# Sixteen groups of zero products put into a fixed order of steps, three taken out

## The chip, the cores and the metric

The kernel runs on one core of a Trainium2 chip. The core has a matrix engine (TensorE, PE in the profile, with its weight loads as PEld), a vector engine (VectorE, DVE), a scalar engine (ScalarE, ACT), a general engine (GpSimd, POOL) and a queue that issues transfers (SyncE, SP). Each works off its own instructions in order and waits on semaphores for the others. The metric is the device time of one execution in microseconds; lower is better, and of several runs the median counts.

## The reference

Two blocks stand behind each other, in float32. The first is a delta rule over 768 steps in time for 4 batches of 8 heads of 48 features; the second mixes over the sequence and then over the channels.

```python
k_n = k / (np.linalg.norm(k, axis=-1, keepdims=True) + 1e-06)
for t in range(S):
    y[:, :, t] = einsum('bhd,bhde->bhe', q[:, :, t], state)
    v_old = einsum('bhde,bhd->bhe', state, k_n[:, :, t])
    state += beta[:, :, t] * outer(k_n[:, :, t], v[:, :, t] - v_old)
x = y.transpose(0, 2, 1, 3).reshape(4, 768, 384)
u = x + (relu(x.transpose(0, 2, 1) @ w_tok1) @ w_tok2).transpose(0, 2, 1)
out = u + relu(u @ w_ch1) @ w_ch2
```

Here w_tok1 is 768x256, w_tok2 256x768, w_ch1 384x1536 and w_ch2 1536x384. They come as 64-bit numbers and are rounded on the core.

## The kernel before

**Tiling.** The recurrence is cut into units of 128 positions of one batch (24 units u), each of two chunks of 64. For each unit the kernel loads keys and queries (job k, `load_kq`), normalises and transposes them (p, `prep`: the transposes are L562 and L582, ScalarE copies them out of PSUM in L566 and L587), forms the products of keys with keys and queries (c and d, `grams`, L511, and their masking on VectorE, L517), inverts a unit triangular matrix of each chunk (t, i, f, h, j: to parts, the elimination on VectorE in L755 and L760, back, and the joining of parts by small products, L790, L803, L864, L905), loads the values (v), and runs the recurrence over the chunks (r, `recur`: L933, L940, L957, L963, L971 and L972, L980, L985). Units 0 to 5 pass the inversion in SBUF; later ones go through DRAM on the way in and out (n_dram and w_dram). Four units share one inversion.

**The second block** is job m for batches 0 and 1 (`mixer`: L1606, L1621, L1681, L1702) and T, A, F, B for batches 2 and 3, which run at the end. The weights are rounded piece by piece (w0 to w33, `round_weights`: a load in L280, ScalarE in L286 and L287, VectorE in L289, GpSimd in L293). Job b loads beta (L252), turns it on TensorE into p_b (L257) and copies it to beta_st on ScalarE (L261).

**The order.** Each job is a Python generator; `next` issues its instructions up to the next yield. What comes when is written out by hand: the string `order` (L1788) is a list of steps, `k0*6` being six steps of job k0, and the loop at L1861 issues them one by one. The tile framework is told to keep this order, so on each engine the instructions stand in the order of the string. A step that waits holds up all that is behind it on its engine.

**Zero products.** Three jobs multiply zeros by zeros into a PSUM tile of their own, p_warm, that nobody reads: x and z take one product of 128x128 by 128 or by 512 columns, Y (and y, the same generator) takes four of 64x64 by 128 columns that lie in the four quarters of the array. In float32 each product is two matmul instructions in the trace, so an x or a z is two and a Y eight.

```python
def keep_warm(m):
    zero = warm[:, 0:128]
    while True:
        nc.tensor.matmul(p_warm[:, 0:m], zero, zero[:, None, :].to_broadcast([128, m, 128]))
        yield
def warm_tiles():
    while True:
        for j in range(2):
            for r in PAR:
                nc.tensor.matmul(p_warm[r, j], warm[r, 0:C], warm[r, 0:128])
        yield
```

Of the kernel before, what the change touches and what calls it, by code (L numbers as in the profile page):

```python
# [23 lines left out]
def kernel(  # L24
# [41 lines left out]
    B, H, S, D = q.shape  # L66
# [117 lines left out]
    t11 = const.tile([128, NB, HB], FP32, name="t11")  # L184
# [17 lines left out]
    w1 = const.tile([128, NCH, DTOK], FP32, name="w1")  # L202
    w2 = const.tile([128, NDH, S], FP32, name="w2")
# [407 lines left out]
    t16 = spare[:, cuts[1] : cuts[2]].rearrange("s (q t b) -> s q t b", q=2, t=QB)  # L611
# [1182 lines left out]
    w13*2 w6*2 k5*2 v0 k6 k5*2 i0*2 d4*2 k5 x z d4*3 c4 z*2 p5*2 k5 t4 p5 h0 h1  # L1794
    h0 w8*2 h1 Y i0 f0 Y p4 f1 h2*2 p5*3 f0*2 w6 h0*5 k6*5 p6 z f2*2 k8*3 p5 w6
    p5 p3 p5 j0*3 f1*2 h1*5 j0*2 w8*2 w17 f2 h2*3 v0 w17 r0*5 p6 h2*2 c5*2 v1
    w11*2 j1 p5 k7*2 c5 k7 c5 r0 c5 r0*2 w14*2 v1 w11*2 k7*2 p7 d5*5 r1*5 w14*2
    p6*2 t5 j1 r1*2 j1 j2 p7 h3*2 r1*3 p6*3 i1*2 r2*5 k8*2 f3*2 w9 k9*3 j1*2 v2*2
    i1*3 j2*2 r2*2 f3 i1*2 p6*3 w16 v2 w16*3 r2*2 h3 r2 i1 d6 r3*5 i1*2 w9*3 v2
    d6 h3 v2 w0 h3*2 r3 h3 d6*2 w0 d6 j3 c6*5 r3*4 w0 j2 w0 p8*2 j2 r4 p8 r4*4  # L1800
    k9*3 j3*2 r4*2 i1*2 w24 i1*2 p7*7 r4 c7 r4 r5*5 k10 p9 k10 p9 c7 r4 c7*3 i1
    w5*2 p7 r5*2 w24*3 r5*3 j3*2 i1 r6*4 w26 v3*5 p9 k11 r6 d7*5 w26*3 p8*3 t6*2
    r6*2 w5*2 p8*4 v4*2 t6 i1 r6*3 h5*2 h4*2 k10*2 f4*3 c8*2 k10 p10 w28*2 c8*2
    r7 c8 r7*3 d8*4 p9 d8 w28 h4*5 p9 t6 r7*2 j4 w28 p9*3 r7*2 p9 w7 d9 w7 v4*2
    f5*2 w27*2 w7*2 d9*4 c9*2 f5 c9*3 t7*2 t8 r7*2 t7*2 j4*2 v4 p10*2 h5 r8*3 w29
    t8*3 w29 w27*2 r8*2 w29*2 q3 w29 j4*2 r8 w22*4 t9*3 r8*3 p9 r9 p10 r9*3 t9 v5
# [36 lines left out]
    m1*2 p23*3 m1*3 p23*5 v18 r29 p22 f18 m1*3 c23*3 f20*2 f18 c23 f18*2 c23
    f19*3 v18 r30 t22*4 c23 t23 r30*4 t23*3 f20 m1*3 i6 j18*3 f19 m1*2 S m1 j19*2
    j20 j19 f21 r29*2 f21 i6*4 m1*3 i6*6 j20*2 m1 r30*3 m1*2 r30*2 i6 f21 m1*2
    r30 r31*4 r28 r30*2 i6 j21 f20 j21*2 i6*2 r31*3 v20 i6 v20*2 i6 m1*2 i6*3
    r31*4 f21 j21 i6*2 v22*3 v20*2 r32*5 r31 r29 r31*2 i6*3 m1*5 j21 m1 r32 v21*2
    r32 i6*7 m1*2 r30 r32*6 v21*2 s v21 s v22 m1*4 v22 s f22 f23 f22*3 r33*5
    f23*2 j22 m1*4 r33*3 v23 j22 r33*2 j22 W j23*2 T2 r33*2 T2 f23 r33 l s l s
    r33 j23 r34*4 j23 r34*2 W*3 v23*4 j23 r34*2 T2 r32 r34*5 r35*8 T2 r35*2 T3 W  # L1850
    r35*2 l*2 T3 s*5 W*2 T2*5 s r34 r35 A0*7 T2*3 A0*11 S*3 A0*6 l s l s A0*18 A1
    A0*4 A1*2 A0*3 S*3 A0*20 A1*2 T3*2 F0*5 T3*10 A1 S T3 A1*3 T3*3 B0 T3*8 B0*3
    T3*4 B0 T3 A1*5 T3*3 A1*2 B0*2 A1*6 W A1*3 F0 A1*6 F0 A1*4 B0 A1*15 A2 F0
    A1*3 A2*2 A1*9 F0*2 A1*14 W*3 A2*3 B0*2 A2*5 B0*3 W*2 F0 B0*3 F1 F0 B0*2 F0*2
    B0 A1 B0*4 F0 F1*2 B0*6 A2*10 B1 F1*2 A2*7 B1 A3*2 A2*3 B0 A2*26 A3 A2*12 F1
    A2*2 F1*4 B1*4 A2*5 A3 F1 F2 A3 B1*4 A3*6 F1*2 B1*7 F1 B1*2 A2 F2*3 F1 B1*6
    B2 A3*10 B1*3 A3*15 B1 A3*26 F2*4 A3*3 F2*3 B1 B2*4 A3*7 B2*5 A3 B2*2 A3*4
    F2*2 F3 B2*7 F3*2 B2*2 F3*2 B2 F3*3 B2*6 F3 F2*2 B3*2 F3 B3*10 F3 B2*2 B3*5
    F3*4 B3*13
    """  # L1860
    for word in order.split():  # L1861
        name, _, n = word.partition("*")
# [34 lines left out]
```

## Time and profile before

| what | value |
|---|---|
| median of three runs | 619.56 us (616.66 to 621.06) |
| the profiled execution | 617.85 us, span 616.1 us |
| mean granted TensorE clock | 0.983 |
| TensorE, VectorE, ScalarE, GpSimd busy | 588.7, 468.3, 253.8, 107.5 us |
| zero products | x36 instructions of x and z (L235), x48 of Y (L245) |
| steps in the order | 2598, of which 8 are x, 10 z, 6 Y |

Three views are used beside the page. A window gives the busy time of every engine in a stretch, the granted clock and the DMA share (the numbers with an x are counts of instructions). The chain of waits goes back from the last instruction to what released it, step by step. The timeline lists instructions in the order of time, with the idle time of the engine ahead of one and what ended it in square brackets: `[1.30 <-PE p_b L257]` is 1.30 us idle, ended by TensorE's p_b. Times in them count from the start of the span. "Cold" is not a word of the profile: the column PEclk has the share of the clock that was granted, and 0.50 is half.

### The profile page before, as it was taken

Reading aid. Unit: us, or ns where it says so; the run is one execution under the profiler, and the core shown is the slowest. Engines: PE = TensorE matmul, PEld = TensorE weight load, DVE = VectorE, ACT = ScalarE, POOL = GpSimd, SP = SyncE. Lnnn points to the kernel's source line nnn. Section 1 sums busy time; section 2 is a strip of 40 time slices with the busy share of each in tenths; the row PEclk is TensorE's granted clock in tenths of the full one; section 3 lists DMA queues with packets and bytes.
Section 4 is the critical chain, followed back from the end, with each engine's and each line's share of the span. In section 5 each row is a group of like instructions: output and inputs, shape, how many; then the busy total and the mean of one; then the engine's idle time right before and its main releaser. Section 6 shows DMA issues by size and latency. Waiting matters only on the chain.

```text
span 616.1 us, 21239 instructions
## 1 busy us (share of the span) xinstructions
PE 588.7 (96%) x8733; PEld 513.6 (83%) x8733; DVE 468.3 (76%) x1506; ACT 253.8 (41%) x676; POOL 107.5 (17%) x144
## 2 busy tenths in 40 slices
PE   9488988999999999999999999999999999999998
PEld 5467775667898988977889898896699999999997
DVE  4996876986799754797567977967788898775874
ACT  7659885457521344222651305424252332414200
POOL 3147364134411112013020120010000000000000
PEclk9979897999999999999999999998999999999999
DMA  9577657647542344354435343144102012020001
GB/s 220 112 160 166 166 145 199 160 115 183 109 110 65 85 106 82 92 122 103 104 71 136 84 99 63 35 87 117 34 0 40 1 22 56 1 53 13 14 27 51
DMA packets 154608, 55.55 MB, mean 90 GB/s; under 512 B 129648, under 2 KB 148976, under 8 KB 154512
## 3 DMA queue, kind: packets, MB, share of 16 engines
q1 hardware_dynamic: 154512, 54.20, 37.9%
q8 instruction: 68, 1.11, 0.8%
q14 instruction: 28, 0.23, 0.1%
HBM read 41.19 MB, written 11.21 MB: 85 GB/s over the span
## 4 chain that ended last, share of the span: by engine, by line
PE 81%; DVE 10%; ACT 5%; issue 2%; DMA 1%; SPq 0%; ACTq 0%; DVEq 0%
PE p_c L1681 16%; PE p_r L1511 13%; PE p_o L1702 13%; PE p_a L1583 7%; PE p_b L1583 6%; PE p_g L511 3%; PE p_h L1621 3%; PE p L1606 2%; DVE sub L755 2%; DVE x L760 2%; PE p L1236 2%; PE p_y L1047 1%; PE p_warm L235 1%; PE p_h L1251 1%; PE p_k L933 1%
## 5 line engine op out<-in xcount | busy, mean ns | idle before, releaser
L1681 PE MATMUL p_c<-u_t,wc 128*128 128x256 f32 x432 | 101.6, 386 | 0.3 <-issue 0.3
L1681 PEld LDWEIGHTS p_c<-u_t,wc 128*128 128x128 f32 x432 | 79.6, 190 | 11.7 <-issue 0.8
L755 DVE TENSOR_TENSOR sub<-x 128x56 f32<-128x56 f32 (+41 forms) x351 | 71.1, 243 | 4.4 <-DMA x<-n_dram 2.3
L760 DVE TENSOR_TENSOR x<-x,sub 128x56 f32<-128x56 f32 (+41 forms) x351 | 69.0, 237 | 0.2
L1702 PE MATMUL p_o<-wc,r 128*128 128x192 f32 x360 | 64.3, 330 | 0.2 <-DVE xb L1641 0.2
L1702 PEld LDWEIGHTS p_o<-wc,r 128*128 128x128 f32 x360 | 58.4, 190 | 1.5 <-DVE xb L1641 0.5
L1690 ACT ACTIVATE r<-p_c 128x512 f32<-128x512 f32 x36 | 21.5, 596 | 52.2 <-PE p_c L1681 46.4
L511 PE MATMUL p_g<-kq 48*64 48x128 f32 (+1 forms) x704 | 33.5, 280 | 3.3 <-ACT kq L587 3.3
L517 DVE TENSOR_TENSOR gm<-p_g,mb 128x512 f32<-128x512 f32 x44 | 28.9, 684 | 7.5 <-PE p_g L511 7.0
L574 POOL TENSOR_TENSOR mb<-mask_c,cs 128x512 f32<-128x512 f32 x20 | 21.4, 1068 | 71.3 <-DVE cs L552 41.7
L484 POOL TENSOR_TENSOR v_st<-v_st,nrm 128x384 f32<-128x384 f32 x12 | 11.3, 944 | 126.5 <-DMA v_st<-in_v_dram 97.7
L293 POOL TENSOR_TENSOR wc<-w_f,d 128x384 uint32<-128x384 uint32 x24 | 24.7, 1031 | 42.2 <-DVE w_f L289 17.0
L511 PEld LDWEIGHTS p_g<-kq 48*64 48x64 f32 (+1 forms) x704 | 25.7, 136 | 6.1 <-ACT kq L587 4.3
L1511 PE MATMUL p_r<-t_d,wc 128*128 128x192 f32 x160 | 28.8, 326 | 0.0
L1524 DVE TENSOR_TENSOR kq<-kq,p_r 128x384 f32<-128x384 f32 x40 | 21.1, 552 | 10.0 <-PE p_r L1511 8.1
L1524 DVE TENSOR_TENSOR gm<-gm,p_r 128x384 f32<-128x384 f32 x40 | 21.1, 552 | 8.1 <-PE p_r L1511 5.8
L1511 PEld LDWEIGHTS p_r<-t_d,wc 128*128 128x128 f32 x160 | 26.5, 190 | 0.0
L400 DVE STREAM_TRANSPOSE kq<-pads 128x512 f32<-128x512 f32 x24 | 25.4, 1105 | 1.0 <-PE p_y L1047 0.6
L1702 PE MATMUL p_o<-wc,s 128*128 128x192 f32 x144 | 25.7, 330 | 0.0
L1511 PE MATMUL p_r<-pads,wc 128*128 128x192 f32 x128 | 25.4, 326 | 0.0
L1702 PEld LDWEIGHTS p_o<-wc,s 128*128 128x128 f32 x144 | 23.3, 190 | 0.6 <-DVE xb L1641 0.3
L1511 PE MATMUL p_r<-t_d,lent 128*128 128x192 f32 x128 | 23.7, 326 | 0.0
(311 smaller groups left out, 1362.2 us busy)
## 6 DMA issues: line engine op xcount, KB each, us to landing
d<-in_moe_w_ch_dram SPq DMA_DIRECT2D x24, 384.0 KB, 3.8
v_st<-in_v_dram SPq DMA_DIRECT2D x96, 48.0 KB, 2.8
out_dram<-xb SPq DMA_DIRECT2D x23, 192.0 KB, 1.9
kst<-in_k_dram SPq DMA_DIRECT2D x64, 48.0 KB, 2.4
n_dram<-gm SPq DMA_DIRECT2D x72, 32.0 KB, 1.7
pads<-in_k_dram SPq DMA_DIRECT2D x24, 96.0 KB, 2.3
pads<-in_q_dram SPq DMA_DIRECT2D x24, 96.0 KB, 3.4
gm<-w_dram SPq DMA_DIRECT2D x72, 32.0 KB, 2.3
```

Of the source, the lines that this page charges most:

```text
L293: nc.gpsimd.tensor_tensor(out=dst.bitcast(U32), in0=f, in1=lo, op=ALU.add)
L400: nc.vector.transpose(kq_of[p // 2][:, i, :, p % 2].rearrange("f p (s g) -> f p g s", g=G), rows_of[i].rearrange("s p (g d) -> s p g d", g ...
L511: nc.tensor.matmul(p_g[PAR[i ^ cc ^ swap(u)], p], kqt[f, p, cc, 0], kqt[f, p, cc])
L517: nc.vector.tensor_tensor(out=blocks(gm_of(u))[:, :, cc, D:GW].rearrange("s p (two n) -> s p two n", two=2), in0=p_g, in1=made[u][:, :, cc ...
L755: nc.vector.tensor_tensor(out=half, in0=by[0].to_broadcast(list(to.shape)), in1=by[1].to_broadcast(list(to.shape)), op=ALU.mult,)
L760: nc.vector.tensor_tensor(out=to, in0=to, in1=half, op=ALU.add)
L1511: nc.tensor.matmul(p[:, i], pieces[q // width][:, at : at + 128], f[f"u{n}"], start=first and i == 0, stop=True, skip_group_check=True,)
L1524: nc.vector.tensor_tensor(out=o, in0=o, in1=p, op=op_of(sign))
L1583: nc.tensor.matmul(p, a[:, i], w[:, i // 2, i % 2], start=first and i == 0, stop=True, skip_group_check=True,)
L1681: nc.tensor.matmul(p_c[:, k], piece_of(wc1, cb, f * 128)[:, f * 128 : (f + 1) * 128], u_t[:, cb], start=(cb == 0), stop=(cb == NCB - 1),)
L1690: nc.scalar.activation(r2[:, m], p_c, ACTF.Relu)
L1702: nc.tensor.matmul(p, a[:, m], wc2[:, m, j], start=(start and i == 0), stop=(i == NM - 1), skip_group_check=True,)
```

## The change

Only the string `order` differs. Among all its steps but x, z and Y the order is the same. One x and one z go from the start, and one z moves a step ahead (counted as one out and one in). Otherwise come in: nine Y, two x, and four z, three of these behind each other. The new order has 2611 steps.

| at about (us in the trace of before) | before | after |
|---|---|---|
| 2 to 4 | `w10 x*4 z w10*2` | `w10 x*3 w10*2` |
| 12 | `p0*2 z w3` | `p0 z p0 w3` |
| 22 | `p3*7 c3` | `p3*6 Y p3 c3` |
| 25 | `i0*2 w13` | `i0*2 z*3 w13` |
| 43 | `i0 f0 Y p4` | `i0 f0 Y*2 p4` |
| 47 | `j0*3 f1*2` | `j0 Y j0*2 f1*2` |
| 50 | `w8*2 w17` | `w8 Y w8 w17` |
| 58 | `p6*3 i1*2` | `p6 Y p6*2 i1*2` |
| 64 | `r2*2 h3` | `r2 Y r2 h3` |
| 69 | `r3*4 w0` | `r3*2 x r3*2 w0` |
| 79 | `d7*5 w26*3` | `d7*4 z d7 w26*3` |
| 94 | `r8*3 w29` | `r8 Y r8*2 w29` |
| 101 | `h5*3 j5` | `h5 x h5*2 j5` |
| 110 | `j5 i2*3 p10` | `j5 Y i2*3 p10` |
| 138 | `f7 m0 w29` | `f7 Y m0 w29` |

In the source the lines of the string are filled anew, so that many of them shift. Its first lines:

```diff
     order = """
-    w10 x*4 z w10*2 z w1*4 k1*3 z k1*3 z b p1 z p1 k0*6 p0*2 b*2 p1 w2 p0*5 p1*2
-    w10 p0*2 z w3 w2 c0*3 p0 w3*2 d0*2 w3 c0 p1 c0 d0*3 k2*3 v1 p1*2 w18 k2*2
+    w10 x*3 w10*2 z w1*4 k1*3 z k1*3 z b p1 z p1 k0*6 p0*2 b*2 p1 w2 p0*5 p1*2
+    w10 p0 z p0 w3 w2 c0*3 p0 w3*2 d0*2 w3 c0 p1 c0 d0*3 k2*3 v1 p1*2 w18 k2*2
     p1*2 c1*2 d1 k2 p2*2 c1 t0 d1 c1*2 d1*3 p2*8 c2*2 w2 d2 c2*3 Y d2 w2 k3*6 p3
-    d2*2 p3 d2 t1 x p3*7 c3 k4*5 k7 w13 w18*2 d3*2 v1*2 v0*2 c3*3 v0 c3 d3*3 p4*2
-    t2 x t3 p4*2 x i0*2 w13 p4*2 w18 w17*2 i0 k4 i0*9 p4 i0*2 p4*2 c4 k8 c4*3
...
+    d2*2 p3 d2 t1 x p3*6 Y p3 c3 k4*5 k7 w13 w18*2 d3*2 v1*2 v0*2 c3*3 v0 c3 d3*3
+    p4*2 t2 x t3 p4*2 x i0*2 z*3 w13 p4*2 w18 w17*2 i0 k4 i0*9 p4 i0*2 p4*2 c4 k8
...
```

More of the change, by code (lines that the diff above doesn't have):

```diff
@@ L1800 @@
[L1800 to L1806, printed above, removed]
@@ L1856 @@
[L1856 to L1859, printed above, removed]
+    d2*2 p3 d2 t1 x p3*6 Y p3 c3 k4*5 k7 w13 w18*2 d3*2 v1*2 v0*2 c3*3 v0 c3 d3*3
+    p4*2 t2 x t3 p4*2 x i0*2 z*3 w13 p4*2 w18 w17*2 i0 k4 i0*9 p4 i0*2 p4*2 c4 k8
+    c4*3 w13*2 w6*2 k5*2 v0 k6 k5*2 i0*2 d4*2 k5 x z d4*3 c4 z*2 p5*2 k5 t4 p5 h0
@@ new lines @@
+    h1 h0 w8*2 h1 Y i0 f0 Y*2 p4 f1 h2*2 p5*3 f0*2 w6 h0*5 k6*5 p6 z f2*2 k8*3 p5
+    w6 p5 p3 p5 j0 Y j0*2 f1*2 h1*5 j0*2 w8 Y w8 w17 f2 h2*3 v0 w17 r0*5 p6 h2*2
+    c5*2 v1 w11*2 j1 p5 k7*2 c5 k7 c5 r0 c5 r0*2 w14*2 v1 w11*2 k7*2 p7 d5*5 r1*5
+    w14*2 p6*2 t5 j1 r1*2 j1 j2 p7 h3*2 r1*3 p6 Y p6*2 i1*2 r2*5 k8*2 f3*2 w9
+    k9*3 j1*2 v2*2 i1*3 j2*2 r2*2 f3 i1*2 p6*3 w16 v2 w16*3 r2 Y r2 h3 r2 i1 d6
+    r3*5 i1*2 w9*3 v2 d6 h3 v2 w0 h3*2 r3 h3 d6*2 w0 d6 j3 c6*5 r3*2 x r3*2 w0 j2
+    w0 p8*2 j2 r4 p8 r4*4 k9*3 j3*2 r4*2 i1*2 w24 i1*2 p7*7 r4 c7 r4 r5*5 k10 p9
@@ new lines @@
+    w4 i2 j5 Y i2*3 p10 v5 r9*2 d10*3 r10 v7*2 j5 i2*2 r10*4 w12 i2 k12 i2*2 m0
+    w32 k11 k12 w32 r10*2 m0 p11 k12*4 w19 p11 r10 c10 r10 c10 r10 w33 d10*2 q2 Y
+    r11*4 v7 r11*3 w19 c10 q1 w30 c10 r11 k12*2 i2*3 r11 v6*4 i2*5 m0*3 i2*5 q5
+    i2 m0 p11*4 c10 p11 m0 p11*2 m0*2 k12*2 w12 m0*3 v6 f6*3 w12 d11 c11*2 d11*2
+    c11 w33 c11 d11*2 j6 p12 w12 m0 w33 w30*3 p12*2 f7*3 j6*2 m0 c11 j7 f6 f8
+    w27*2 f8 j7 f8 w15 f7 Y m0 w29 w33 w29 j7 r12*4 w31 j8 p11 t10*3 r12 Y r12 f9
+    j8 f9 w21 p12 r12 f8 r13*2 w15*2 r12 w15 r13*3 w31*3 Y r13*2 w33 j8 w21 m0
@@ new lines @@
+    r13 q4 p12*4 r13*2 m0*2 r14 c12 f9 j9 r14*2 w21 t10 w20*2 v7 r14*2 c12*2 w33
+    c12 r14 v8 c12*2 r14*2 w25*2 j9 r14 r15 v8 w21 r14 r15 w25 r15*3 w25 k13*4
+    w20 k13*4 p13 k13*2 w20 v8*3 m0*2 p13 w25 p13 m0 r15 p13 r15 p13 w27 w25
+    k13*2 j9 m0*4 p13 f9 w23 t12*3 p13 t12 w25 r15*3 c13*6 w23 k14*7 r16*5 m0 p13
+    m0*3 w23*4 k14 r16*2 t11 t13*2 j9*2 t11*3 w33 p14 r16*2 p14*2 w31 m0*3 w31 m0
+    w31 m0 w23 r17*2 r16 t13 r17 t13 r17*2 p14*2 m0*2 p14 i3 k14*4 i3*3 k15 v9*2
+    m0*3 v10 i3*5 k15 i3 r17 k15*2 p14 k15*3 m0 v10*2 i3 k15*2 m0*2 k15*2 i3*4
@@ new lines @@
+    r17*4 k15 i3*2 p14 m0*2 i3*6 m0*4 r18 i3 r18*2 v9*3 r18*2 i3*8 m0*10 v10*2 m0
+    r18 c14*4 r18*2 m0*2 f10 c14 f10*2 f12*2 p15*3 m0*4 r18 r19 r18 r19*3 j10 f10
+    j10*2 f12 p15 f11*4 f12 r19 c14 r19 v11 p15*3 k16*7 j11 m0*2 r19*4 j11 j12
+    r20*3 k16*2 r20 m0 r20 k16*3 v11 m0 j11 r20*2 v11*2 p15 c15*2 p10 r20*2 c15
+    r20 c15*3 f13*3 p16 r21*5 m0 r21*2 p16*4 k17*7 p16 j12*2 p16 k17 r21*3 m0*3
+    r22 c16 r22*3 k17*4 v11 r22 c16*4 r22*2 m0 r22 t14 p17 f13 c16 t14 j13*2 t14
+    r22 r23 t15*2 t16 r23*2 r22 r23 m0*3 r23 t15*2 r23 p17*5 t16 p17 j13 t16*2
@@ new lines @@
+    r27*2 p20*2 k20*2 p20 c19*2 r26*2 k20 v16*2 r25 c19 m1*2 f17 r27*4 p20 k20
+    p20 j17*2 m1 r27*5 c20*4 p20 r28*4 c20*2 k21*9 p21*2 k21*2 p21 k21 m1*2 v16
+    r28 t18 v17 p21*5 t19*4 t18*2 j17 t18 j17 m1*2 r28*3 c21*6 m1*3 r28*3 m1*2
+    r28 m1 t20 s t20*3 t21*4 i5 m1*4 i5 v17*2 r26 i5*2 m1*2 r28 k22*3 i5*4 k22*6
+    m1*2 i5*2 m1*3 i5 v17 r29 i5*3 p22*2 i5 r29 v17 r29*3 i5*2 v19 p22*3 k22*3
+    m1*4 r29 v19*2 i5 k23*6 p22 v18 p22 i5*11 k23*4 r29*2 k23 i5 k23 v18*2 i5*2
+    v19 m1*7 v19 m1*5 r29 c22*5 r29 r27 c22 m1*2 p23*3 m1*3 p23*5 v18 r29 p22 f18
@@ new lines @@
+    m1*3 c23*3 f20*2 f18 c23 f18*2 c23 f19*3 v18 r30 t22*4 c23 t23 r30*4 t23*3
+    f20 m1*3 i6 j18*3 f19 m1*2 S m1 j19*2 j20 j19 f21 r29*2 f21 i6*4 m1*3 i6*6
+    j20*2 m1 r30*3 m1*2 r30*2 i6 f21 m1*2 r30 r31*4 r28 r30*2 i6 j21 f20 j21*2
+    i6*2 r31*3 v20 i6 v20*2 i6 m1*2 i6*3 r31*4 f21 j21 i6*2 v22*3 v20*2 r32*5 r31
+    r29 r31*2 i6*3 m1*5 j21 m1 r32 v21*2 r32 i6*7 m1*2 r30 r32*6 v21*2 s v21 s
+    v22 m1*4 v22 s f22 f23 f22*3 r33*5 f23*2 j22 m1*4 r33*3 v23 j22 r33*2 j22 W
+    j23*2 T2 r33*2 T2 f23 r33 l s l s r33 j23 r34*4 j23 r34*2 W*3 v23*4 j23 r34*2
@@ new lines @@
+    T2 r32 r34*5 r35*8 T2 r35*2 T3 W r35*2 l*2 T3 s*5 W*2 T2*5 s r34 r35 A0*7
+    T2*3 A0*11 S*3 A0*6 l s l s A0*18 A1 A0*4 A1*2 A0*3 S*3 A0*20 A1*2 T3*2 F0*5
+    T3*10 A1 S T3 A1*3 T3*3 B0 T3*8 B0*3 T3*4 B0 T3 A1*5 T3*3 A1*2 B0*2 A1*6 W
+    A1*3 F0 A1*6 F0 A1*4 B0 A1*15 A2 F0 A1*3 A2*2 A1*9 F0*2 A1*14 W*3 A2*3 B0*2
+    A2*5 B0*3 W*2 F0 B0*3 F1 F0 B0*2 F0*2 B0 A1 B0*4 F0 F1*2 B0*6 A2*10 B1 F1*2
+    A2*7 B1 A3*2 A2*3 B0 A2*26 A3 A2*12 F1 A2*2 F1*4 B1*4 A2*5 A3 F1 F2 A3 B1*4
+    A3*6 F1*2 B1*7 F1 B1*2 A2 F2*3 F1 B1*6 B2 A3*10 B1*3 A3*15 B1 A3*26 F2*4 A3*3
@@ L1860 @@
+    F2*3 B1 B2*4 A3*7 B2*5 A3 B2*2 A3*4 F2*2 F3 B2*7 F3*2 B2*2 F3*2 B2 F3*3 B2*6
+    F3 F2*2 B3*2 F3 B3*10 F3 B2*2 B3*5 F3*4 B3*13
     """
```

69 lines of the change are left out of this document (14 added, 55 removed).

## The prediction

> **What bounds the kernel now.** I read the page first, then busy time by stage, the chain of waits, and last the rows around each place where a group of zero products comes or goes.
>
> ```profile
> PE 588.7 (96%) x8733; PEld 513.6 (83%) x8733; DVE 468.3 (76%) x1506; ACT 253.8 (41%) x676; POOL 107.5 (17%) x144
> PE 81%; DVE 10%; ACT 5%; issue 2%; DMA 1%; SPq 0%; ACTq 0%; DVEq 0%
> 17.30:47.50 30.20, 21.16 (x310) 15.67 (x302) 28.63 (x99) 17.67 (x46) 10.96 (x11) 0.89 0.61 132
> 47.50:57.00 9.50, 8.24 (x311) 7.76 (x312) 4.64 (x12) 8.83 (x27) 7.14 (x11) 1.00 0.85 207
> 57.00:94.20 37.20, 33.52 (x1062) 29.07 (x1059) 31.00 (x110) 32.67 (x88) 19.76 (x25) 0.95 0.65 154
> 94.20:102.30 8.10, 5.21 (x117) 4.28 (x118) 3.11 (x10) 3.90 (x11) 4.86 (x5) 0.79 0.60 179
> 102.30:113.80 11.50, 10.53 (x178) 6.82 (x177) 11.24 (x59) 7.03 (x18) 1.74 (x3) 0.85 0.66 150
> 113.80:616.00 502.20, 495.20 (x6639) 440.31 (x6639) 381.65 (x1189) 170.58 (x454) 58.44 (x74) 1.00 0.32 74
> ```
>
> The last six rows are stretches; behind length and comma stand the busy times of PE, PEld, DVE, ACT and POOL, then the granted clock. From 113.8 us on TensorE is busy 495.2 of 502.2 us: whatever is put in its queue there costs its full length. Before that it isn't the bound: VectorE is busy 28.63 of 30.20 us up to 47.5, ScalarE 8.83 of 9.50 up to 57, both with TensorE in turns up to 94.2, then a round trip through DRAM, then VectorE 11.24 of 11.50. There a zero product is free as long as TensorE would have waited, and a full clock is worth only what others wait for TensorE.
>
> ```profile
> 27.30:30.71 3.41, 0.00 (x0) 0.00 (x0) 3.34 (x18) 1.52 (x4) 1.04 (x1) 1.00 0.76 172
> 30.71:37.54 6.83, 4.64 (x32) 3.28 (x32) 6.80 (x48) 2.57 (x5) 1.54 (x3) 0.50 0.95 202
> ...
> 47.78:51.19 3.41, 2.44 (x112) 2.17 (x107) 1.61 (x5) 3.24 (x10) 2.49 (x4) 1.00 0.79 183
> ...
> 58.02:61.43 3.41, 2.75 (x106) 2.32 (x107) 3.31 (x11) 3.27 (x9) 2.22 (x3) 1.00 0.52 101
> 61.43:64.85 3.42, 3.42 (x86) 3.00 (x80) 3.13 (x23) 2.46 (x7) 0.17 (x1) 0.50 0.77 201
> ...
> 95.57:98.98 3.41, 1.48 (x54) 1.09 (x57) 0.84 (x3) 2.31 (x7) 2.54 (x3) 1.00 0.17 29
> 98.98:105.81 6.83, 6.39 (x51) 4.32 (x43) 4.74 (x27) 2.98 (x10) 1.83 (x3) 0.50 1.01 299
> ...
> 423.25:426.66 3.41, 2.59 (x97) 2.17 (x98) 2.48 (x7) 0.99 (x4) 0.00 (x0) 1.00 0.12 29
> 426.66:430.07 3.41, 3.41 (x28) 1.72 (x29) 3.31 (x8) 0.42 (x1) 0.00 (x0) 0.50 0.02 5
> ```
>
> The clock falls to half four times, for 6.83, 3.42, 6.83 and 3.41 us, each time behind a stretch of 3.41 us in which TensorE did little. The three early dips lie in the part that the change edits, the fourth does not.
>
> **The change part by part.** The order of all other steps is kept, so no other instruction and no DMA moves past another; SP and POOL have the same queues, and TensorE's alone gains and loses products. The sum is made against the profiled execution (617.85 us, span 616.1); the median of the runs is 619.56, 1.71 more, and I carry the sum over as a difference.
>
> *One x and one z fewer at the start.*
>
> ```profile
> 1.05 8.27 PE p_warm L235 x18
> 9.32 1.53 PE p_b L257 x47
> 4.05 0.55 ACT L286 ACTIVATE d<-d 128x384 f32<-128x384 f32 x1 [1.83 <-DMA d<-in_moe_w_ch_dram]
> 9.05 0.52 ACT L539 ACTIVATE ksq<-kst 128x384 f32<-128x384 f32 x1
> 10.88 0.50 ACT L261 COPY beta_st<-p_b 128x192 f32<-128x192 f32 x1 [1.30 <-PE p_b L257]
> L257 PEldq EVENT_SEMAPHORE  x1: 51/51/51, 6.9 to 6.9; - x1
> 1.05:2.92 1.87, 1.87 (x8) 1.87 (x9) 1.00 0.54 112
> 2.92:6.34 3.42, 3.42 (x6) 1.35 (x6) 1.00 1.08 293
> 7.01:9.25 2.24, 2.24 (x6) 0.76 (x4) 1.00 1.03 270
> ```
>
> TensorE works off 18 zero products (4 x, 5 z, two instructions each) before p_b, whose own wait is over at 6.9. So p_b stands behind the zeros, and ScalarE behind p_b: idle 1.30 us, then busy without a break. The speeds: 8 products of 128 columns in 1.87 us is 0.47 for an x; four of 512 start within 3.42 us (the row's six count the tail of an x and the next head), 1.71 for a z; from 7.01 on five in 2.24, 0.90 for a z. So the clock came up near 6.8 (the column shows 1.00 as no record precedes it). What goes is 0.43 to 0.47 + 1.71 us of slow work; the slow time is filled either way, so the queue ends earlier by half of it, 1.07 us. ScalarE would be free at 9.57, 1.31 earlier, and so takes all 1.07. Bounds: 0, if a load behind it sets the pace anyway, and 1.30, ScalarE's idle time. I take 1.07, since the ScalarE work behind it and VectorE's from 17.3 have almost no idle time to swallow it.
>
> *Groups before 47 us.* The z moved by one step passes a step that issues a copy on ScalarE only: 0. The Y in p3 falls into a TensorE wait, as the three z behind i0*2 do in part:
>
> ```profile
> 25.56 0.60 PE L562 MATMUL p_t<-ident,pads 128*128 128x128 f32 x4
> 32.23 1.09 PE L582 MATMUL p_t<-ident,pads 128*128 128x128 f32 x4 [6.07 <-DMA pads<-in_q_dram]
> 28.26 0.56 ACT L566 COPY kq<-p_t 128x512 f32<-128x512 f32 x1
> 28.09 1.17 DVE x L731
> ...
> 47.60 0.69 PE L864 MATMUL p_z<-t,wc 32*32 32x32 f32 x32 [0.29 <-DVE t L826]
> 48.91 0.74 ACT L882 COPY zst<-p_z 32x256 f32<-32x256 f32 x2
> ```
>
> The three z (2.7 us) stand ahead of the transposes at 25.56 and push their end to 28.9; ScalarE's copy waits some 0.6 us, and the load of the next keys into that buffer, queued on SP behind the transposes, as much. The 6.07 us wait for the q load hides the rest; on ScalarE and SP the cover is the slack of later loads, and the chain of waits runs through VectorE's first inversion, from 28.09 on: 0. If the cover were gone: 0.6. They leave about 3.3 us of idle time ahead of 32.23, so I let the first dip stand; it costs nothing, as VectorE sets the pace there. The second Y at f0 and the Y in j0 delay TensorE by 0.44 each ahead of j0's product (47.60), less 0.29 of waiting: up to 0.6. That product ends at 48.29 and its reader on ScalarE starts at 48.91, in-order behind a copy: slack 0.62. I take 0, bounds 0 and 0.6.
>
> *Groups from 47 to 114 us.*
>
> ```profile
> 50.80 0.92 PE L803 MATMUL p_x<-gm,z 64*48 64x48 f32 x32 [0.41 <-ACT wc L808]
> 59.00 0.67 PE L933 MATMUL p_k<-ss_t,wc 48*64 48x48 f32 x16 [0.47 <-DVE ss_t L980]
> 63.10 0.59 ACT L587 COPY kq<-p_t 128x512 f32<-128x512 f32 x1 [0.72 <-PE p_t L582]
> 62.02 1.06 PE p_t L582 x4
> 46.71 0.60 PE L582 MATMUL p_t<-ident,pads 128*128 128x128 f32 x4
> 80.45 0.25 PE L957 MATMUL p_w<-rw_t,gm 64*64 64x48 f32 x1 [0.69 <-DVE rw_t L940]
> 113.77 0.23 PE L957 MATMUL p_w<-rw_t,gm 64*64 64x48 f32 x1 [0.22 <-DVE rw_t L940]
> 116.99 0.44 PE p_warm L245 x8
> ```
>
> A Y (eight products of 64x64) takes 0.44 us of TensorE. The one in w8 falls into the wait of 0.41, the one in p6 into that of 0.47: 0 each. The z in d7 (0.90) has a wait of 0.69 behind it: 0 to 0.2. The Y in r2, the x in r3 (0.2) and the Y in r8, the x in h5 stand behind products whose readers were served, and ahead of copies that queue on a busy ScalarE or of the DRAM round trip: together 0.1, bounds 0 and 1.3 (all of 2 x 0.44 + 2 x 0.2). The Y behind j5 has a wait of 0.22 and interleaved products to hide in: 0.1, bounds 0 and 0.44.
> What they may give: the Y in p6 puts 0.44 us of products into the stretch 58.02 to 61.43, the fullest (2.75 us) of the four that led to a dip. While the clock is low ScalarE waits 0.72 us for transposes that took 1.06 instead of 0.60. Without the dip 0.46 of it goes, and about 0.15 of the products before them: −0.6, bounds 0 and −0.72. I take −0.6. The dip at 98.98 I let stand: no group falls between 95.57 and 98.98.
> The Trainium skill, "TensorE: Matmul & The Clock Gate", section "What's actually happening", says that the clock goes to half after an idle window of about 3.4 us. The trace agrees at 30.71 and differs at 61.43, where TensorE was busy 2.75 of 3.41 us; by that rule eight small products change nothing there, and the sum below would be −0.4.
>
> *Y behind f7 (138 us).* TensorE is the bound and goes on with the mixer: +0.44, bounds 0.2 and 0.51 (what seven of eight took at 140).
>
> **Sum:** −1.07 + 0 + 0 + 0.1 + 0.1 − 0.6 + 0.44 = −1.03. From 619.56: **618.5 us** (616.8 for a profiled execution like this one).
>
> **The rivals.**
> - *The dip at 61 stays.* For it: the stretch 47.78 to 51.19 had 2.44 us of products, less than the 2.75, and no dip followed, so the busy share doesn't decide alone and 0.44 more may not matter. Then −0.43: 619.1 us. The page's rule named above asks for this outcome.
> - *Slower: the groups are not covered between 42 and 97 us.* ScalarE and TensorE take turns there, and a product delayed is a copy delayed. Exposed would be the second Y at f0, those in j0, w8, p6, r2 and r8 (6 x 0.44), the x of r3 and h5 (0.4) and the z of d7 (0.9): 3.9 us. With −1.07 and +0.54 behind it: +3.4, 623.0 us. It decides from about 0.5 us exposed if the dip stays, 1.1 if it goes. Against it: the waits of 0.29 to 0.69 us just quoted, which stand at four of these places (j0, w8, p6, d7).
> - *More comes of the clock.* If the three z also end the first dip, and TensorE is late there for VectorE, its 4.64 busy us at half clock shrink by 2.3: 618.5 − 2.3 = 616.2. For it: the z fill 2.7 of the 6.07 us. Against: VectorE is busy 6.80 of 6.83 us in that dip.
> - *The start gives nothing,* as loads in the first 16 us set the pace: 618.5 + 1.07 = 619.6. For it: the DMA share in the rows of the start is 1.03 to 1.08. Against: of ScalarE's waits up to 28 us only the first, ended at 4.05, is for a DMA.
>
> **How the numbers follow.** Forecast 0.38; dip at 61 stays 0.22; slower 0.16; more of the clock 0.14; start gives nothing 0.10. The time is that of the likeliest, 618.5. The range goes from 615.0 (616.2 less 1.2, as the three runs shown lie 1.5 to 2.9 from their median) to 621.6, which holds the first, second and last with such a scatter and the lower half of the slower one. Likeliest alone: 616.5 to 620.3. A measurement of this kernel can tell about 1% (6.2 us) from no change; no case alone reaches that: beyond 613.4 only if the clock gives more than all I have priced, 0.05; beyond 625.8 only if all groups are exposed and the start gives nothing, 0.04; within, 0.91.
>
> **What would show it.** Right: p_b near 8.2 us and ScalarE's beta_st near 9.8; VectorE's first inversion near 27.0; full clock from 61 to 65; the last wait before TensorE is the bound at about 112.3 instead of 113.8; some 0.44 more zero products behind it. Wrong: ScalarE waiting for DMA in the first 16 us, new TensorE releases of 0.3 us or more ahead of ScalarE's copies at 47 to 97, or dips in other places than before, which would move the time by the length of each wait that they make.

## The result, and the profile after

Twenty runs of each kernel give 622.54 us (617.49 to 626.87) for the changed one and 620.49 (614.69 to 623.27) for the one before: medians 2.05 us apart. The ratio over the fast runs (one of the changed kernel's was slow) is 1.0051 with a 95% interval of 1.0027 to 1.0075. By the ratio the change makes the kernel slower by some 3 us (1.7 to 4.7), half a per cent; forecast were 1 us the other way and a range that ends at 621.6. The profiled execution took 622.63 us, its span is 620.9.

The page of the changed kernel: busy times, the clock by slices (section 2), the instruction transfers (section 3), the shares of the chain of waits (section 4) and the costliest group (section 5; behind the bar: busy time, mean ns of one, and the idle time ahead of them with what ended it).

```profile
PE 594.5 (96%) x8813; PEld 518.8 (84%) x8813; DVE 469.9 (76%) x1506; ACT 254.1 (41%) x676; POOL 105.4 (17%) x144
...
PEclk9978898999999999999999999999999999999999
...
q8 instruction: 69, 1.13, 0.8%
...
PE 77%; DMA 7%; DVE 7%; ACT 4%; SPq 2%; issue 2%; POOL 0%; DVEq 0%; ACTq 0%
...
L1681 PE MATMUL p_c<-u_t,wc 128*128 128x256 f32 x432 | 101.5, 386 | 1.7 <-issue 1.7
```

The last row is the one to hold on to: the mixer's products lie in the stretch that TensorE bounds, they wait for nobody, and yet TensorE stood still ahead of them for 1.7 us, released by "issue", that is by nothing that the profile shows. The kernel before has the same row with another end, and so has the group L859 of both kernels, in the list of groups by line, first the kernel before:

```profile
L1681 PE MATMUL p_c<-u_t,wc 128*128 128x256 f32 x432 | 101.6, 386 | 0.3 <-issue 0.3
...
L859 PE MATMUL p_z<-gm,zst 32*32 32x32 f32 x416 | 10.0, 198 | 0.6 <-issue 0.6
```

then the changed one:

```profile
L859 PE MATMUL p_z<-gm,zst 32*32 32x32 f32 x416 | 10.2, 198 | 0.8 <-issue 0.8
...
L864 PE MATMUL p_z<-t,wc 32*32 32x32 f32 x64 | 1.6, 193 | 1.0 <-issue 1.0
```

Where the 4.8 us between the two spans come from is read by laying the same instruction of both traces side by side (start in the changed kernel less start in the one before, TensorE):

| at, us (before) | 44 | 52 | 56 | 58 | 64 | 70 | 130 | 138 | 150 | 300 | 320 | 435 to the end |
|---|---|---|---|---|---|---|---|---|---|---|---|---|
| later by, us | -0.69 | -0.48 | +0.28 | +0.54 | +3.08 | +2.90 | +2.60 | +4.08 | +3.46 | +2.94 | +5.05 | +4.78 |

Two steps stand out, between 54 and 64 us and between 300 and 320. (The 1.5 us between 130 and 138 are, for the most part, a wait of 0.8 us for VectorE at 135 and the Y behind f7.) At each TensorE stops, by 1.02 us in the joining products of j1 and by 1.73 us in the mixer; the timeline of the changed kernel has both:

```profile
55.89 0.32 PE L864 MATMUL p_z<-t,wc 32*32 32x32 f32 x9 [1.02 <-issue]
...
312.23 1.56 PE L1681 MATMUL p_c<-u_t,wc 128*128 128x256 f32 x6 [1.73 <-issue]
```

Behind the first the clock is at half for three windows instead of the one of before; around the second TensorE was busy 2.27 of 4.00 us. Busy time by stretch in the changed kernel (PE, PEld, DVE, ACT, POOL, then the clock):

```profile
57.91:68.15 10.24, 10.24 (x218) 9.24 (x213) 7.24 (x35) 7.15 (x19) 2.84 (x4) 0.50 0.49 112
...
309.00:313.00 4.00, 2.27 (x124) 2.02 (x117) 1.08 (x1) 2.53 (x9) 0.24 (x1) 1.00 0.53 124
```

and in the kernel before, in 8 us around the same instructions, without a gap:

```profile
305.00:313.00 8.00, 8.00 (x273) 6.90 (x272) 4.49 (x10) 5.16 (x17) 2.87 (x4) 1.00 0.55 122
```

**What a stop is.** TensorE has 8813 products and 8813 weight loads in the changed kernel, and the queue q8 carried 69 packets of instructions, 1.13 MB: 17626 instructions, with 136 more that only wait on semaphores or drain 17762, over 69 packets are 257 for each, 64 bytes apiece (before: 17602 over 68 are 259), so about 256. Counting all of them from the start of a trace and dividing by 256 gives each its place in such a block. The 18 traces of this study have 99 stops of over 0.15 us that end in "issue", and all of them have the same fraction, 0.754 to 0.762. So they stand where one block ends and the next begins. The transfer queues around the stop at L1681, from 309.56 to 310.74 us (the row of q8) and from 310.8 to 313.4, where only q1 has a row:

```profile
q8 instruction: 1, 0.02, 6.1%
...
q1 hardware_dynamic: 793, 0.19, 36.3%
```

The packet is on its way from 309.57 to 310.72 us; TensorE has run out of instructions at 310.50 and goes on at 312.23, 1.51 us after the packet landed. Between the landing of a packet and the end of a stop lie 1.08 to 1.67 us at each of the 99; at the 1121 boundaries without a stop the block begins 1.14 us or more behind its packet's landing, half of them over 4.6. So no block was begun sooner than about 1.1 us after its packet had landed. A block that TensorE works off in less time than its successor takes to come leaves it with nothing to do. Here the packet set out 0.90 us after the block ahead of it began, took 1.16 to land and 1.51 more to be of use, 3.57 us together, and TensorE was through with that block in 1.83: the difference is the stop. All 99 stops stand behind one of the 480 blocks that took under 5.1 us, none behind the 740 longer ones. The Trainium skill, "Runtime: NRT & Kernel Launch", section "Instruction fetch mechanics", says that engines fetch in blocks of 256 instructions and that the crossing of a boundary is mostly hidden; the blocks agree with these traces, and "hidden" holds for most of the 69 and not for those that cost here 0.2 to 2.1 us.

With that a theory for the loss can be stated: the change adds 160 TensorE instructions (nine Y of 16 with their weight loads, four z and two x of four, less one x and one z; the sixteenth added group is the z moved by a step), so from 138 us on every block begins 160 instructions earlier in the work, and its ends fall on other, denser stretches. (The block ahead of the stop at L1681 took 1.83 us, the one ahead of that at L859 2.50; the blocks of the same numbers in the trace of before took 3.31 and 4.41.) Rivals: added products that are not covered by waits; a clock that goes to half at more or at worse places.

### The profile page after: what moved, and what is told of

It is laid out like the page before. It is cut to its first block, busy times and chain, and to the rows that moved or that the text cites. A ratio compares the mean times of both kernels' runs of the same rounds, so it can differ in the third digit from the quotient of the medians.

```text
span 620.9 us, 21399 instructions
## 1 busy us (share of the span) xinstructions
PE 594.5 (96%) x8813; PEld 518.8 (84%) x8813; DVE 469.9 (76%) x1506; ACT 254.1 (41%) x676; POOL 105.4 (17%) x144
## 3 DMA queue, kind: packets, MB, share of 16 engines
q8 instruction: 69, 1.13, 0.8%
## 4 chain that ended last, share of the span: by engine, by line
PE 77%; DMA 7%; DVE 7%; ACT 4%; SPq 2%; issue 2%; POOL 0%; DVEq 0%; ACTq 0%
PE p_c L1681 15%; PE p_r L1511 13%; PE p_o L1702 11%; PE p_a L1583 6%; PE p_b L1583 6%; PE p_g L511 3%; PE p L1606 2%; PE p_k L933 2%; PE p_h L1621 2%; PE p_h L1251 1%; DVE sub L755 1%; PE p_y L1047 1%; DVE x L760 1%; PE p_s L971 1%; DMA x<-n_dram 1%
## 5 line engine op out<-in xcount | busy, mean ns | idle before, releaser
L1681 PE MATMUL p_c<-u_t,wc 128*128 128x256 f32 x432 | 101.5, 386 | 1.7 <-issue 1.7
L1681 PEld LDWEIGHTS p_c<-u_t,wc 128*128 128x128 f32 x432 | 79.6, 190 | 13.1 <-issue 2.4
L1702 PE MATMUL p_o<-wc,r 128*128 128x192 f32 x360 | 64.6, 331 | 0.8 <-DVE xb L1641 0.8
```

Of the source, the lines that this page charges most:

```text
L1681: nc.tensor.matmul(p_c[:, k], piece_of(wc1, cb, f * 128)[:, f * 128 : (f + 1) * 128], u_t[:, cb], start=(cb == 0), stop=(cb == NCB - 1),)
L1702: nc.tensor.matmul(p, a[:, m], wc2[:, m, j], start=(start and i == 0), stop=(i == NM - 1), skip_group_check=True,)
```

## The experiments

All ratios are against the kernel before, run beside it on the same chip; the 95% interval stands behind them.

**Each part alone.** The diff of the order in four parts.

```diff
 e1_open
-x*4 z w10*2          ... p0*2 z w3
+x*3 w10*2            ... p0 z p0 w3
 e2_to50
-p3*7   i0*2 w13      f0 Y p4     j0*3       w8*2
+p3*6 Y p3   i0*2 z*3 w13   f0 Y*2 p4   j0 Y j0*2   w8 Y w8
 e3_58to79
-p6*3        r2*2 h3      r3*4          d7*5
+p6 Y p6*2   r2 Y r2 h3   r3*2 x r3*2   d7*4 z d7
 e4_94to138
-r8*3        h5*3        j5 i2*3     f7 m0
+r8 Y r8*2   h5 x h5*2   j5 Y i2*3   f7 Y m0
```

> Only the start of the change: one x and one z fewer, the z of step 12 one step earlier; all other groups as before. Every theory that takes the start at its word (forecast, exposed groups, clock) expects -1.1 us against before, 0.998, with beta_st near 9.8 us. Blocks theory (TensorE stops once per 256 of its instructions while the next block is fetched, and fewer or more zero products move the place of the stops): eight TensorE instructions fewer move every stop by eight instructions, so the sum may differ from -1.1 by one or two stops of 0.5 to 1.5 us, either way, and the idle times put down to issue should again stand at one and the same position of the blocks.

> Only the groups up to 50 us: Y in p3, three z behind i0*2, a second Y at f0, Y in j0, Y in w8; the start as before. Forecast (covered): 0 to +0.2 us. Exposed groups: +0.6, as the changed kernel lost 0.3 us at 47 and 0.3 at 51 in its trace. Clock: the first dip shortens or not, no time from it, the dip at 58 or 61 stays; blocks: +-1 us beside that, 60 instructions more.

> Only the groups of 58 to 79 us: Y in p6, Y in r2, x in r3, z in d7. Forecast: -0.6 us, as the dip at 61 goes. Dip stays: 0 to +0.3. Exposed groups: +1.0 to +1.9 (0.44 to 0.88 for each Y, 0.2 for the x, up to 0.9 for the z; more where the clock is at half). Clock: the length of the dip between 57 and 69 decides, 3.4 us of half clock being worth about 1 us.

> Only the groups from 94 us on: Y in r8, x in h5, Y behind j5, Y behind f7. Forecast: +0.5 to +0.6 us (0.44 of the last, 0.1 of the third). Exposed groups: +1.0 to +1.5, all four at their full length. Blocks: the stops behind 94 us move, +-1 us.

Measured: 0.9980 (0.9956 to 1.0003), 1.0010 (0.9983 to 1.0037), 0.9978 (0.9949 to 1.0007), 1.0006 (0.9981 to 1.0031). Together that is -0.0026, or -1.6 us, where the whole change gives +0.0051; the sum of four such ratios is uncertain by some 0.005. No part shows the loss; it seems to be in something that the parts have only together. The stops in their traces stood at places of their own (64.6 us 1.58 in the first; 423.2 us 1.19 in the second; 143.7 us 1.36 in the third; 416.0 us 1.15 in the fourth), which is what turned the attention to blocks: each part moves them by another number, -8, 76, 40 and 52.

**The changed kernel again, and twice with other products in one wait.** At i0*2 the three z (12 instructions) give way to six Y (96 instructions) or thirteen x (52); and six Y alone are put there in the kernel before.

```diff
 e6_after_6Y:   -i0*2 z*3 w13   +i0*2 Y*6 w13
 e7_after_13x:  -i0*2 z*3 w13   +i0*2 x*13 w13
 e8_before_6Y:  -i0*2 w13       +i0*2 Y*6 w13
```

> The changed kernel once more, unaltered, to see whether its +0.5% is a property of the kernel. All theories: 1.003 to 1.007 against the kernel before. What a second trace can tell: if the loss is where TensorE's instruction blocks end, its stops with nothing to wait for stand at the same instructions as in the first trace (near 55.9, 146, 312 and 421 us). If the loss is an unlucky clock in the first trace alone, the ratio falls to 1.000.

> The changed kernel with its three new z at i0*2 (3 x 0.9 = 2.7 us, 12 TensorE instructions) replaced by six Y (6 x 0.44 = 2.64 us, 96 instructions). The idle time that they fill is 6 us long, so nothing else is later or earlier; but all TensorE instructions behind them stand 84 places further in the blocks of 256. If the loss comes from where blocks end: the stops stand at other instructions, 84 earlier, and the time differs from the changed kernel by 1 us or more, most likely downward (1.000 against before). If it comes from added products that are not covered, or from the clock: the same time as the changed kernel, 1.005 against before.

> The same with thirteen x (13 x 0.2 = 2.6 us, 52 instructions) for the three z: behind them all stands 40 places further in the blocks. If the loss comes from where blocks end: another time than the changed kernel by 1 us or more, and another than with six Y. If from products not covered, or the clock: 1.005, as the changed kernel.

> The kernel before with six Y alone at the place of the three z (behind i0*2), 96 instructions of TensorE in a 6 us wait: nothing is exposed. If where blocks end matters: the time moves by 1 us or more from the kernel before, in either direction (stops of 1.2 us near 98 and 0.5 near 146 give way to others). If only exposure and the clock matter: 1.000 within 0.002.

Measured: again 1.0059 (1.0034 to 1.0084); six Y 1.0098 (1.0068 to 1.0129); thirteen x 1.0060 (1.0025 to 1.0096); before with six Y 1.0026 (0.9997 to 1.0055). The loss belongs to the kernel. In its second trace the two large stops stood at the same instructions, and the first of them was followed by a window at half clock (timeline, then busy time by stretch):

```profile
309.14 2.29 PE L1681 MATMUL p_c<-u_t,wc 128*128 128x256 f32 x6 [1.85 <-issue]
...
418.41 0.21 PE L859 MATMUL p_z<-gm,zst 32*32 32x32 f32 x1 [1.03 <-issue]
```

```profile
309.83:313.24 3.41, 3.41 (x73) 2.58 (x75) 0.35 (x1) 1.25 (x3) 0.67 (x1) 0.50 0.50 112
```

The other three decide little. With six Y and thirteen x the stops did go to other instructions (none near L1681 with six Y; with thirteen x 1.38 us at L856, 310.58 us, beside four others behind 140 us, 4.06 us in all), but the times did not move as expected: the one rose, the other stayed. The six Y were a poor stand-in besides, since the mean granted clock fell to 0.977 from 0.983 in the changed kernel: why is not shown, as the kernel before with the same six Y had 0.984. A test had to move the blocks behind the part that the clock plays with, and back to a place that is known.

**The blocks put back, and the blocks moved alone.** A tiny product of zeros n, 32x32 by 32 columns, is four TensorE instructions. 24 of them are 96, and 96 + 160 = 256: in the changed kernel they put every later block back where the kernel before has it. 40 of them are 160: in the kernel before they put the blocks where the changed one has them. They stand in TensorE's waits at 95 to 112 us.

```diff
+    t32 = (slice(0, 32), 0, slice(0, 32))
+    w32 = warm[0:32, 0:32]
+    jobs["n"] = (nc.tensor.matmul(p_warm[t32], w32, w32) for _ in iter(int, 1))
 e9_after_24n, against the changed kernel
-j4*2 r8 w22*4 t9*3 r8*3        i2*2 r9 w4
+j4*2 n*8 r8 w22*4 t9*3 r8 n*8 r8*2    i2*2 n*8 r9 w4
 e10_before_40n, against the kernel before: the same places with n*16, n*12, n*12
 e11_open_2n, against the kernel before: the opening of e1_open, and
-i0*2 w13
+i0*2 n*2 w13
```

> The changed kernel with 24 tiny products of zeros (32x32, some 0.04 us each, eight in each of three TensorE waits of 0.7 to 1.0 us between 98 and 112 us): 96 TensorE instructions, which with the 160 of the change make 256, so that from 138 us on every instruction has the place in its block that it has in the kernel before. Theory (an instruction packet that lands late): the stops at L1681 near 312 us (1.73 and 1.85 in two traces) and at L859 near 420 us (0.78 and 1.03) are gone, those of the kernel before come in their place (L972 146 us 0.5, L859 224 us 0.6, L1681 389 us 0.3), and the time falls by 1.5 to 2.5 us from the changed kernel, to 1.002 against before. Rivals (products not covered; the clock): 1.005, as the changed kernel, and the stops stay where they were in time.

> The kernel before with 40 such products (1.7 us) in three TensorE waits between 95 and 109 us: 160 instructions, as many as the change adds, so that from 138 us on its blocks begin where those of the changed kernel do. Nothing else of the change is in it. Theory: stops of about 1.8 us at L1681 near 311 us and of 0.8 to 1.0 at L859 near 419 us appear, those at 224 and 389 us go; slower than before by 1.5 to 2.5 us, ratio 1.003 to 1.004. Rivals: 1.000 within 0.002, since the products fill waits.

> The opening alone (one x and one z fewer, one z moved), with two tiny products in the 6 us wait at i0*2 that give back the eight instructions taken away, so that every block behind it is as before. By the prediction's first term -1.07 us: ratio 0.998. If the start gives nothing: 1.000. Theory of the blocks: the stops are those of the kernel before (87, 98, 146, 224, 389 us), not those of the opening alone (64.6 us 1.58, 70.1 us).

> The kernel before once more, against itself: a ratio of 1.000 within 0.0025, which says what the intervals are worth, and a second trace of it. Theory of the blocks: its stops stand at the same instructions as in the first trace (L957 98 us 1.19, L972 146 us 0.54, L859 224 us 0.63, L1681 389 us 0.29), and none stands near 311 us; if stops are chance, they stand elsewhere.

Measured: 1.0017 (0.9991 to 1.0042); 1.0054 (1.0023 to 1.0084); 0.9981 (0.9957 to 1.0006); the kernel before against itself 1.0014 (0.9981 to 1.0048). Expected were 1.002 and 1.003 to 1.004 for the first two. The kernel before, without any part of the change, loses about as much time as the changed one when its blocks begin at the same instructions, and its stops behind 114 us are then those of the changed kernel. The groups by line of e10_before_40n:

```profile
L1681 PE MATMUL p_c<-u_t,wc 128*128 128x256 f32 x432 | 101.5, 386 | 1.8 <-issue 1.8
...
L859 PE MATMUL p_z<-gm,zst 32*32 32x32 f32 x416 | 10.2, 200 | 1.1 <-issue 1.1
```

and of e9_after_24n, the changed kernel with its blocks put back:

```profile
L1681 PE MATMUL p_c<-u_t,wc 128*128 128x256 f32 x432 | 101.6, 386 | 0.5 <-issue 0.5
...
L859 PE MATMUL p_z<-gm,zst 32*32 32x32 f32 x416 | 9.9, 198 | 0.0
```

Its 0.5 us at L1681 is the stop that the kernel before has at 389 us. Not all that was expected came. In the second trace of before the stops at L1681 (0.54) and, with 0.14, at L859 stood where they had; those at L957 (98 us) and L972 (146 us) did not, and L856 had one of 1.13 at 142 us. e9 lacks the one at 224 us. The opening alone with its blocks held had 0.32 at 98 us and 0.54 at 146, but also 1.61 at 64.9, which was to be gone, and none at 87, 224 and 389. So the place of a block says where a stop can stand, not that there is one.

Side by side with the trace of before, e10 is 0.67 us ahead at 130 us and 0.66 at 300 (its stop at 143 us and the other's at 224 cancel between them), and 1.24 behind at 320. Over these 20 us (300 to 320) the four traces with the changed kernel's blocks fall back by 2.11, 3.45, 3.62 (the changed kernel) and 1.89 us (e10), half clock behind the stop included; a second trace of before, e11 and the three traces with blocks put back (e9, and e13 and e14 below) by -0.02 to 0.32.

The times of e9 are not as clean as they look. The clock averaged 0.979 in e10, 0.986 in e9, 0.983 in the changed kernel and 0.982 in the one before. Over the 133 runs of the kernel before beside these experiments 0.001 less of clock goes with 0.5 us more; by that, an estimate, e9 at the clock of before would be 3.6 us slower than it (1.2 measured, as a difference of means) and e10 1.8 (2.8 measured). So the changed kernel's own loss is not a low clock, but what e9's time gained came with a higher one; that the clock is higher because the stops are gone is not shown (below). Nor do its 24 products look free: between 97 and 115 us the three traces that have them fall back by 3.6 to 5.4 us against the trace of before, those of the changed kernel by 0.3 to 1.5 and e10 with its 40 by 0.3. All three have half the clock there, beginning between 111.9 and 113.5 us; in e9:

```profile
111.88:118.71 6.83, 6.68 (x93) 4.47 (x88) 6.73 (x30) 1.58 (x5) 1.03 (x2) 0.50 0.69 152
```

e9's trace, besides, is that of the longest of its twelve runs (623.90 us). The case for the blocks rests on e10 and on the places of the stops; that e9 came out at its expected 1.0017 is in part luck.

**The three Y between 42 and 52 us.** They are taken out of e9's kernel; twelve n in the wait at i0*2 keep the later blocks in place. Beside it e9's kernel again, a third trace of the changed one, and the two parts that had done best, with 54 n to give them the blocks of e1_open.

```diff
 e13_no_3Y, against e9_after_24n
-i0*2 z*3 w13        f0 Y*2    j0 Y j0*2   w8 Y w8
+i0*2 z*3 n*12 w13   f0 Y      j0*3        w8*2
 e15_open_58to79_54n: e1_open and e3_58to79 together, and
-i0*2 w13
+i0*2 n*54 w13
```

> The changed kernel with the 24 tiny products of before, and without the three Y between 42 and 52 us (the second at f0, those in j0 and w8); twelve more tiny products in the 6 us wait at i0*2 keep every block from 52 us on where it was. If these three groups are not covered (in the changed kernel's first trace the lead over the kernel before shrinks from 1.1 to 0.5 us between 44 and 52 us): 0.6 us less than the same kernel with the three Y, and more if the clock gains by it. If they are covered, as the prediction had it: no difference. The stop at L864 near 55.8 us (1.02) stays in both cases, since its block begins at the same instruction.

> The changed kernel with the 24 tiny products once more, for comparison on the same chip with the run without the three Y, and for a second trace: 1.000 to 1.003 against the kernel before; stops at L864 near 55 us and at L1681 near 390 us, none at L1681 near 312 us or L859 near 420 us.

> What did best so far put together: the opening and the groups of 58 to 79 us, with 54 tiny products in the 6 us wait at i0*2, so that from 79 us on the blocks begin where they did with the opening alone, whose trace had the fewest stops behind 114 us (0.34 and 0.20). If the parts add up when the blocks are held: 0.995 to 0.997 against the kernel before, the opening's 1.1 us, the groups' 1 us and some 0.9 us of stops. If the opening's gain is all there is: 0.998.

> A third trace of the changed kernel. Theory of the blocks: stops at L864 5.754 blocks from the start, at L856 20.754, at L1681 42.758 (1.7 to 1.9 us) and at L859 57.758 again. Where the clock goes to half will differ from the first two.

Measured: 1.0012 (0.9980 to 1.0044) without the three Y, 1.0023 (0.9985 to 1.0061) with them; the two parts with 54 n 1.0004 (0.9969 to 1.0038), no gain; one run of the changed kernel, 625.98 us. The times cannot tell the three Y from nothing. The traces can, in two ways. Between 41.5 and 51.9 us four traces with them lose 0.27 to 0.56 us on the one without (0.56 and 0.41 the first two of the changed kernel, 0.27 and 0.54 those with the 24 n; the third of the changed kernel has half the clock from 39 to 46 us and is left out). And the stop at L864, expected to stay, is gone. Its group in e13_no_3Y, and then in e14_after_24n_again:

```profile
L864 PE MATMUL p_z<-t,wc 32*32 32x32 f32 x64 | 1.4, 192 | 0.0
```

```profile
L864 PE MATMUL p_z<-t,wc 32*32 32x32 f32 x64 | 1.6, 193 | 0.5 <-issue 0.5
```

All five traces with the three Y have that stop (1.02, 0.47, 0.47 in the changed kernel, 1.02 and 0.47 with the 24 n), the one without hasn't. They are 48 of the instructions ahead of it and take little time, so the block is through in 4.0 us instead of 5.4; the place of the block alone does not make a stop. In the third trace of the changed kernel the two stops behind 300 us are there again, with half the clock behind the first (the one at L856, 146 us, is not); timeline, then busy time by stretch:

```profile
312.82 1.22 PE L1681 MATMUL p_c<-u_t,wc 128*128 128x256 f32 x2 [2.13 <-issue]
...
422.02 0.21 PE L859 MATMUL p_z<-gm,zst 32*32 32x32 f32 x1 [1.13 <-issue]
```

```profile
312.36:315.78 3.42, 2.96 (x10) 1.96 (x14) 0.00 (x0) 0.43 (x2) 0.00 (x0) 0.50 0.59 135
```

The two parts with 54 n had four stops between 57 and 71 us (0.86, 0.64, 0.80, 0.98) and half the clock behind them; 0.995 to 0.997 had been expected: parts whose medians were lower alone did not add up, and no version came out that beats both kernels by more than the intervals.

**The stops behind 114 us, trace by trace** (those over 0.1 us, worked out as said above; in brackets the block):

```
blocks as in the changed kernel                                            sum
 changed, first    L856 0.53 (20)  L1681 1.73 (42)  L859 0.78 (57)  L1065 0.18   3.22
 changed, second   L856 1.00 (20)  L1681 1.85 (42)  L859 1.03 (57)               3.88
 changed, third                    L1681 2.13 (42)  L859 1.13 (57)  L1051 1.41   4.67
 e10_before_40n    L856 1.17 (20)  L1681 1.78 (42)  L859 1.15 (57)               4.10
blocks as in the kernel before
 before, first     L972 0.54 (20)  L859 0.63 (30)   L1681 0.29 (52) L1047 0.14   1.60
 before, second    L856 1.13 (19)  L859 0.14 (30)   L1681 0.54 (52) L1047 0.20   2.01
 e9_after_24n      L972 0.55 (21)  L1681 0.49 (53)  three small 0.43             1.46
 e14, the same                                      L1681 0.30 (53)              0.30
 e13_no_3Y         L972 0.28 (21)  L859 0.26 (31)   L1681 0.55 (53)              1.08
```

The means are 3.97 and 1.29 us: 2.7 us of standing still that the change brings and, but for the Y behind f7, without touching anything there. (In the last three rows the blocks are one whole block further, hence the numbers 21, 31 and 53 for 20, 30 and 52.) The whole way from 115 us to the end says the same: against the first trace of before the upper four lose 2.0, 4.3, 3.7 and 2.5 us there, the other four below -2.3 to 1.4.

## Why the prediction was wrong, step by step

*The opening, -1.07: right.* TensorE begins p_b at 8.1 us (8.2 was forecast). ScalarE's beta_st stands at 9.75 us instead of 10.88, VectorE's first inversion at 26.90 instead of 28.09:

```profile
9.75 0.50 ACT L261 COPY beta_st<-p_b 128x192 f32<-128x192 f32 x1
26.90 1.24 DVE L731 STREAM_TRANSPOSE x<-r 128x1024 f32<-128x1024 f32 x1
```

The wait of 1.30 us for p_b is gone, as the step said. Alone, with the blocks held, it gave 0.9981, -1.2 us, with an interval that reaches from -2.7 to +0.4. The rival that the start gives nothing is made unlikely by the traces, not excluded by the times.

*Groups before 47 us and in j0 and w8, 0: too low by some 0.4.* The traces with and without the three Y differ by 0.27 to 0.56 us, inside the bounds of 0 to 0.6 that were given. The waits of 0.29 to 0.41 us did not cover three groups one behind the other.

*Groups in p6, r2, r3, d7, r8, h5 and behind j5, 0.2: not contradicted.* In the changed kernel's second trace, which has no half clock between 37 and 98 us, TensorE is ahead of the first trace of before by 0.84 us at 54, 0.79 at 75 and 0.94 at 130 us. In between it has two stops of 0.47 and 0.76 us and the other kernel a dip worth 0.6, so little is left for the groups themselves. The rival that the groups from 42 to 97 us are exposed, 623.0 us, names nearly the measured time and is still not the cause: it wanted 3.9 us there, where this trace loses nothing.

*The dip at 61 goes, -0.6: the step was not a difference between the kernels.* Half the clock came at 57.9 to 68.2 us in the first trace of the changed kernel, nowhere between 47 and 98 in the second and third, at 61.4 to 64.8 in the first trace of before and at 50.8 to 54.2 in its second. Where a window of 3.41 us begins differs from execution to execution, so one trace's dip was priced as if it belonged to the kernel. The Trainium skill, "TensorE: Matmul & The Clock Gate", section "What's actually happening", says that the window runs freely and that the phase at the start changes from run to run; these traces agree: counted in lengths of 3.41 us from the start of the span, the first half clock behind the start-up begins 3.40 and 3.02 us into one in the two traces of before, 3.29, 2.62 and 1.75 in the three of the changed kernel.

*Y behind f7, +0.44: right.* TensorE falls back by 0.6 us there in all three traces (+3.50 to +4.08 in the first), more than the bound of 0.51, of which 0.2 come back behind the next zero products.

*What the sum had no term for, and where it failed.* "The order of all other steps is kept, so no other instruction and no DMA moves past another" is true and was taken to mean that nothing behind 138 us changes but by the length of what is added. But TensorE's instructions come in packets of 256, and 160 more of them move all later boundaries. So what moved stops behind 138 us cost was put at nothing. The trace of before had them: six, 3.0 us together, the largest of 1.19 us at 98 us, in the same place of a block as all the others. The prediction quoted the chain's "issue 2%", some 12 us of which they are a part, and did not ask what it was. With 2.7 us for the stops, 0.4 for the three Y and the 0.6 of the dip taken back, -1.03 becomes +2.7, inside the measured +1.7 to +4.7 us (0.27% to 0.75% of the 620.49 us of before). That the sum fits does not prove each of its terms.

*What stays open.* What the change does ahead of 115 us. There the three traces of the changed kernel stand at +2.77, -0.94 and +4.42 us against the first of before, the second of before at -0.71: early stops and half clock differ more from execution to execution than the loss is large. Then, how much of the loss is the clock that follows a stop. Of the nine stops of over 0.75 us behind 300 us in the four traces with the changed kernel's blocks, five had half the clock begin within 0.7 us of their end, which costs 1.7 us of product time each (half of 3.41); of the five traces with the blocks of before three had one dip each between 400 and 440 us, without such a stop. That would be another 1.1 us on the mean of four traces against five, too few to settle. And whether between 54 and 70 us the stop at L864 brings the half clock: it did so with 1.02 us twice and not with 0.47 three times.

## What to carry to other kernels

Before pricing an edit that adds instructions to a bounding engine, list its idle times that end in "issue": if they stand at one place of each block of 256 instructions, every later boundary moves with the edit, and what that costs or gives cannot be read from the edit itself. In a kernel whose bounding engine is fed small products, a change of under 1% is then worth testing with its count of instructions held, by filling up with tiny ones in a wait until the balance is a multiple of 256; that the filler itself costs nothing has to be read from the traces too, as the 24 products of e9 show. And a drop of the clock that one trace shows belongs to that execution until a second trace shows it at the same instructions.

## What the runs showed of the hardware that had not been expected

TensorE can stand still for up to 2.13 us for an instruction packet in the middle of a stretch that is limited by TensorE; in the 99 stops seen work went on 1.08 to 1.67 us after the packet had landed, and at no other of 1220 boundaries did a block begin sooner than 1.14 us behind the landing. Such a stop, in a place where the engine had been busy without a gap, can be followed by 3.41 us at half the clock (0.50 from 309.83 to 313.24 us). Forty tiny products in the waits of one place of the program moved stops that lie 200 and 310 us later.
